# Attention product with two heads of both softmaxes in the rows, high and low factors in the columns, and its halves added in memory

## The chip, the core and the metric

One Trainium2 chip, one NeuronCore of it. The engines run their own instruction queues and meet at semaphores: TensorE (PE; its weight loads are PEld), VectorE (DVE), ScalarE (ACT), GpSimd (POOL) and SyncE (SP). DMAs are issued here by SyncE and by GpSimd. The metric is the device time of one execution in microseconds (us), the median of the runs.

## What is computed

Two blocks over the same x (2048 tokens, 1024 features), mixed by a gate per token. Block A is linear attention with 32 heads of 32 features; the feature map of a head is two softmaxes, of its projected query (or key) and of the negative. Block B is a gated MLP.

```
def _A_ref(x, wqkv, w_phi, wo):
    qkv = (x @ wqkv).reshape(B, S, 3, H, Dh).transpose(2, 0, 3, 1, 4)
    q, k, v = qkv[0], qkv[1], qkv[2]
    pq = einsum("bhsd,hdf->bhsf", q, w_phi); pk = einsum("bhsd,hdf->bhsf", k, w_phi)
    phi_q = concatenate([softmax(pq), softmax(-pq)], axis=-1)
    phi_k = concatenate([softmax(pk), softmax(-pk)], axis=-1)
    kv = einsum("bhsf,bhsd->bhfd", phi_k, v)
    z  = einsum("bhsf->bhf", phi_k)
    num = einsum("bhqf,bhfd->bhqd", phi_q, kv)
    den = einsum("bhqf,bhf->bhq", phi_q, z)[..., None] + 1e-6
    return (num / den).transpose(0, 2, 1, 3).reshape(B, S, D) @ wo
def _B_ref(x, w_gate, w_up, w_down):
    return (gelu(x @ w_gate) * (x @ w_up)) @ w_down
g = sigmoid((x * gate_w).sum(-1, keepdims=True))
return g * _A_ref(...) + (1 - g) * _B_ref(...)
```

## The kernel before

All matrix products work on float32r operands split into a high and a low part (`high` on ScalarE, `low` on VectorE, lines 420 to 424). A product takes three passes, high·high, high·low and low·high (`PASSES`), so 12 matmuls of 128x128 weights by 512 columns make a contraction of 512.

The program has three stages. The first (0 to some 460 us) makes keys and values, their feature map, and the sums `kv` and `z` of each head, which go to memory as `kz`. `finish_kv` (line 238) and `finish_z` (line 255) lay them out by partitions. The second, the *unit stage* (from 463 to 1691 us), makes everything that the last stage multiplies by `wo` and `w_down`: the gated MLP products (`left_mlp`) and the attention result (`left_att`). The third (from 1691 us, line 1088) multiplies those and adds up the output.

The unit stage handles the 2048 tokens in two halves. Gate, up and folded query weights are taken in pairs of 128 columns, and each pair is one *unit* of kind "g", "u" or "q": 30 units in the first half, 32 in the second. A unit is a seven-product scheme for a 2x2 block product (`unit`, line 765): seven products k = 0 to 6 of 12 matmuls. `mine.insert` (line 542) says where the query units stand among the others: in the first half before the change at places 2, 9, 16 and 23 (`7 * m + 2`). The results of a unit are taken out of PSUM at fixed slots after it (`results`, line 747); those of "u" and "q" units go through one of three `hidden` tiles (line 476) to memory by a DMA of GpSimd (`spill`, line 133, and line 732).

The order of instructions on TensorE, VectorE, ScalarE and SyncE is written out by a planner in the program text. `run_slot` (line 450) is called once behind each product. It has a budget of VectorE and ScalarE time per slot (`SLOT` = 2.65 us, plus 1.0 where an attention product was put in, less 0.6 of ScalarE for moves) and emits pieces of *streams*: Python generators that yield (not before slot, due slot, VectorE cost, ScalarE cost). A piece that is due is emitted whatever the budget; others are emitted while budget is left. A piece with a due slot of `NEVER` comes last.

Attention is such a stream without due slots (`attention`, line 838, called from `background`, line 817). For each of 32 *products* (half, group g of four heads, block j of 512 tokens) it loads the projected query from memory (`load_query`, line 831, one DMA of SyncE), transposes 32x32 blocks so that the features of a head lie along the free dimension, takes max and min, subtracts, applies Exp with scale 1 and -1 on ScalarE (line 872), sums, divides by the denominator and the gate, transposes back, and splits into high and low (`pts`). For j = 0 it also builds the block-diagonal factor `kbs` of the four heads from `kz`. `between` interleaves the sums of x for the second half and its reload (`second_half`).

The matmuls of a product are put into `fillers` and issued behind product k = 1 or k = 4 of a unit (line 801 on, in `unit`): `attend` (line 902) multiplies the block-diagonal factors of the two softmaxes by the two halves of `pts`, in three passes each, into one PSUM tile `misc`, evicts it into a `hidden` tile on ScalarE, and spills it to `left_att`. `free[0]` is False from the time a product is handed to `fillers` until it is issued; the stream waits for it before it overwrites `pts`, and, for j = 0, before it overwrites `kbs` (one buffer). What is left of the streams behind the last unit is emitted by `drain` (line 621), ahead of the third stage.

The first stage's and the third stage's loops are the same before and after, but for the layout of `kv` and `z`.

Of the kernel before, what the change touches and what calls it, by code (L numbers as in the profile page):

```python
# [16 lines left out]
P = 128  # L17
# [14 lines left out]
def tile_gated_mix(ctx: ExitStack, tc: tile.TileContext, x, xT, wkT, wqT, wv, w_phi, wo,  # L32
# [33 lines left out]
    for j in range(4):  # L66
        nc.vector.memset(mask[32 * j:32 * j + 32, j, :], 1.0)
    logit = keep.tile([P, S // P], F32, name="logit")
# [77 lines left out]
    with tc.tile_pool(name="kw", bufs=1) as kw, tc.tile_pool(name="kp", bufs=1) as kp, \  # L146
# [91 lines left out]
        def finish_kv(hh, pkv):  # L238
# [10 lines left out]
            for h in range(4):  # L249
                q = h % 2  # L250
                nc.scalar.activation(kv_c[32 * h:32 * h + 32, 4 * hh:4 * hh + 4],
                                     by_head[32 * q:32 * q + 32, :, h // 2, :, q], AF.Copy)
            yield

        def finish_z(hh, s, zacc, pz):
            nc.tensor.matmul(pz, ones, zacc[:, s].rearrange("p h f -> p (h f)"), start=True, stop=True)
            z4 = pz.rearrange("p (g h f) -> p g h f", g=4, h=4)
            for h in range(4):
                q = slice(32 * h, 32 * h + 32)
                nc.scalar.activation(zb[q, 4 * hh:4 * hh + 4, s], z4[q, :, h, :], AF.Copy)  # L260
# [177 lines left out]
    with tc.tile_pool(name="xa", bufs=1) as xa, tc.tile_pool(name="fp", bufs=1) as fp, \  # L438
# [5 lines left out]
        SLOT, NEVER = 2.65, 10 ** 9  # L444
# [227 lines left out]
        start(weights(0, 0, "g", 1))  # L672
# [92 lines left out]
        def unit(n, half, kind, m, before):  # L765
# [6 lines left out]
            for k in range(7):  # L772
# [30 lines left out]
                run_slot(7 * n + k, 1.0 if fill else 0.0, 0.6 * (moved + fill))  # L803
# [27 lines left out]
        def load_query(half, g, j):  # L831
            nc.sync.dma_start(work[:, 4], query[half][g][j])
            if j == 0:
                shared["z"] = fp.tile([P, 2, 2, 32], F32, tag="kz", name="kz", bufs=1)
                for i in range(2):
                    nc.sync.dma_start(shared["z"][:, i], kz[i][:, g])

        def attention(jobs, between):
# [4 lines left out]
            while more:  # L843
# [4 lines left out]
                e, f, x = blocks(e2), blocks(f2), work[:, 7].rearrange("p (a b) -> p a b", b=32)  # L848
                if j == 0:
                    while not free[0]:  # L850
                        yield now[0] + 1, NEVER, 0.0
                    yield now[0], NEVER, 0.5
                    kb = fp.tile([P, 2, 4, 32], F32, tag="kb", name="kb", bufs=1)
                    for s in range(2):
                        nc.vector.tensor_tensor(kb[:, s], z[:, 0, s:s + 1, :].to_broadcast([P, 4, 32]), mask, OP.mult)
                    kbs = shared["kbs"] = fp.tile([P, 2, 2, P], F32R, tag="kbs", name="kbs", bufs=1)
                    kb2 = kb.rearrange("p s a b -> p s (a b)")
                    high(kbs[:, 0], kb2)
                yield now[0], NEVER, 2.1
                nc.vector.transpose(work[:, 7], work[:, 4])  # L860
                mm = fp.tile([P, 2, 16], F32, tag="mm", name="mm", bufs=1)
                nc.vector.tensor_reduce(mm[:, 0, :], x, AX.X, OP.max)
                nc.vector.tensor_reduce(mm[:, 1, :], x, AX.X, OP.min)
                yield now[0], NEVER, 1.6
                if j == 0:
                    low(kbs[:, 1], kb2, kbs[:, 0])
                kbs = shared["kbs"]
                nc.vector.tensor_tensor(e, x.unsqueeze(1).to_broadcast([P, 2, 16, 32]),
                                        mm.unsqueeze(3).to_broadcast([P, 2, 16, 32]), OP.subtract)
                yield now[0] + 1, NEVER, 0.0, 2.0  # L870
                for s in range(2):
                    nc.scalar.activation(e2[:, s], e2[:, s], AF.Exp, scale=1.0 - 2 * s)  # L872
                st = fp.tile([P, 4, 2, 16], F32, tag="st", name="st", bufs=1)
                r, t, d, k = (st[:, i] for i in range(4))
                yield now[0] + 1, NEVER, 1.5
# [5 lines left out]
                yield now[0], NEVER, 2.0  # L881
                nc.vector.tensor_tensor(t, t, r, OP.mult)
                nc.vector.scalar_tensor_tensor(d[:, 0], t[:, 0], 1e-6, t[:, 1], OP.add, OP.add)
                nc.vector.reciprocal(d[:, 0], d[:, 0])
                c = 8 * half + 4 * j
                nc.vector.tensor_tensor(d[:, 0], d[:, 0], g_at[:, c:c + 4].rearrange("p c q -> p (c q)"), OP.mult)
                nc.vector.tensor_tensor(k, r, d[:, 0:1, :].to_broadcast([P, 2, 16]), OP.mult)
# [4 lines left out]
                pts = fp.tile([P, 2, 2, BLK], F32R, tag="pts", name="pts", bufs=1)  # L892
                nc.vector.transpose(wide[1], wide[0])
                yield now[0] + 1, NEVER, 0.0, 1.05
                high(pts[:, 0], f2)
                more = bool(jobs) and now[0] > jobs[0][0] and not (between and now[0] >= between[0][0] - 7)
                if more:
                    load_query(*jobs[0][1:])
                yield now[0] + 1, NEVER, 1.25
                low(pts[:, 1], f2, pts[:, 0])  # L900

                def attend(half=half, g=g, j=j, kbs=kbs, pts=pts):
                    po = misc()
                    for s in range(2):
                        for i, (a, q) in enumerate(PASSES):
                            nc.tensor.matmul(po, kbs[:, a, s, :], pts[:, q, s, :], start=s == 0 and i == 0,  # L906
                                             stop=s == 1 and i == 2)
                    h = hidden()
                    nc.scalar.activation(h, po, AF.Copy)
                    spill(h, left_att[half], j, g)  # L910
# [4 lines left out]
                fillers.append(attend)  # L915

# [257 lines left out]
```

## Time and profile before

| | us |
|---|---|
| median of three runs | 2383.89 (2383.17 to 2384.68) |
| the profiled execution, its time | 2383.34 |
| its span, first to last instruction | 2381.5 |
| unit stage, 467 to 1691 us: TensorE busy | 1222.98 |
| the same: VectorE, ScalarE, GpSimd busy | 897.80, 617.67, 133.25 |
| granted TensorE clock | 1.00 throughout |

Each row of a group names line, engine, operation, output<-inputs, shapes and count, then busy time and the mean of one in ns, then the idle time of the engine ahead of it and what ended that. A row of the timeline has start and length in us. A row of waits reads "who <- for whom: us in total, times, longest". Lengths of matmuls hold their modelled end, so the distance of two starts is what a matmul takes of TensorE.

### The profile page before, as it was taken

The numbers are of one execution on the slowest core, as the hardware profiler recorded it, in microseconds if no ns is written. First come the engines' busy times: TensorE is split into PE (matmuls) and PEld (weight loads), VectorE is DVE, ScalarE is ACT, GpSimd is POOL, SyncE is SP. The second block draws the span as 40 slices with busy tenths as digits, with TensorE's granted clock in tenths as the row PEclk, the third lists the DMA queues.
The fourth block names the chain that finished last, engine by engine and source line by source line (L and its number), as shares of the span: only waits on it lengthen the run. The fifth ranks groups of instructions, "written<-read, shape, count | busy, mean of one in ns | idle before, by whom it ended". The sixth has DMA issues, their size and how long they took to land.

```text
span 2381.5 us, 28170 instructions
## 1 busy us (share of the span) xinstructions
PE 2372.2 (100%) x10689; PEld 1969.3 (83%) x10689; DVE 1746.3 (73%) x2183; ACT 991.6 (42%) x1286; POOL 142.2 (6%) x266
## 2 busy tenths in 40 slices
PE   9999999999999999999999999999999999999999
PEld 8888888788888888888888888888888888888887
DVE  7877868858777777777767676777574878777773
ACT  4323332435445444555555555555443222323221
POOL 0000000011111121110001000000000000000000
PEclk9999999999999999999999999999999999999999
DMA  5112333544444556474444444444685767978774
GB/s 179 47 47 84 98 115 100 180 174 146 179 170 149 194 199 229 171 254 140 138 133 158 142 134 133 153 138 135 240 292 182 252 223 264 327 260 316 261 267 135
DMA packets 154360, 425.10 MB, mean 179 GB/s; under 512 B 21360, under 2 KB 21360, under 8 KB 154224
## 3 DMA queue, kind: packets, MB, share of 16 engines
q1 hardware_dynamic: 127872, 336.64, 42.6%
q0 software_dynamic: 25312, 86.52, 9.4%
q8 instruction: 84, 1.38, 0.2%
q14 instruction: 52, 0.43, 0.1%
q10 hardware_dynamic: 1040, 0.13, 0.0%
HBM read 328.34 MB, written 94.90 MB: 178 GB/s over the span
## 4 chain that ended last, share of the span: by engine, by line
PE 79%; DVE 0%; ACT 0%; issue 0%; ACTq 0%; DVEq 0%
PE po L1088 29%; PE a L744 21%; PE c L744 14%; PE b L744 7%; PE p L744 7%; PE misc L906 2%; DVE x L1048 0%; ACT L872 0%; DVE x L888 0%; DVE tyz L424 0%; ACT x L872 0%; DVE st L876 0%; DVE x L879 0%; ACT tyz L421 0%; DVE v L424 0%
## 5 line engine op out<-in xcount | busy, mean ns | idle before, releaser
L200 PE MATMUL pd<-wkv,x 128*128 128x512 f32 x1536 | 361.3, 392 | 0.0
L200 PEld LDWEIGHTS pd<-wkv,x 128*128 128x128 f32 x1536 | 284.8, 188 | 58.1 <-issue 1.0
L1088 PE MATMUL po<-tw,wgu 128*128 128x512 f32 x1344 | 309.8, 389 | 0.0
L1088 PEld LDWEIGHTS po<-tw,wgu 128*128 128x128 f32 x1344 | 252.3, 188 | 52.4
L421 ACT ACTIVATE wgu<-stage 128x1024 fp32r<-128x1024 f32 x147 | 155.2, 1057 | 291.0 <-PE po L1088 225.1
L424 DVE TENSOR_TENSOR wgu<-stage,wgu 128x1024 fp32r<-128x1024 f32 x147 | 179.6, 1222 | 123.7 <-ACT wgu L421 123.5
L424 DVE TENSOR_TENSOR tyz<-stage,tyz 128x1024 fp32r<-128x1024 f32 x126 | 153.0, 1215 | 41.8 <-ACT tyz L421 41.8
L421 ACT ACTIVATE tyz<-stage 128x1024 fp32r<-128x1024 f32 x126 | 132.7, 1053 | 115.6 <-DVE stage L569 64.3
L744 PE MATMUL a<-s,tyz 128*128 128x512 f32 x744 | 179.4, 390 | 0.9 <-DVE tyz L424 0.4
L744 PE MATMUL a<-x,wgu 128*128 128x512 f32 x744 | 178.7, 389 | 0.0
L744 PE MATMUL p<-s,tyz 128*128 128x512 f32 x744 | 178.7, 389 | 0.0
L744 PE MATMUL c<-x,wgu 128*128 128x512 f32 x744 | 178.7, 389 | 0.0
L744 PE MATMUL b<-s,tyz 128*128 128x512 f32 x744 | 178.7, 389 | 0.0
L744 PE MATMUL c<-x,tyz 128*128 128x512 f32 x744 | 178.7, 389 | 0.0
L744 PE MATMUL a<-s,v 128*128 128x512 f32 x744 | 178.7, 389 | 0.0
L744 PEld LDWEIGHTS a<-s,tyz 128*128 128x128 f32 x744 | 139.4, 188 | 31.0 <-DVE tyz L424 1.3
L744 PEld LDWEIGHTS p<-s,tyz 128*128 128x128 f32 x744 | 139.6, 188 | 29.1
L744 PEld LDWEIGHTS a<-x,wgu 128*128 128x128 f32 x744 | 139.6, 188 | 29.0
L744 PEld LDWEIGHTS c<-x,tyz 128*128 128x128 f32 x744 | 139.6, 188 | 29.0
L744 PEld LDWEIGHTS c<-x,wgu 128*128 128x128 f32 x744 | 139.6, 188 | 29.0
L744 PEld LDWEIGHTS a<-s,v 128*128 128x128 f32 x744 | 139.6, 188 | 29.0
L744 PEld LDWEIGHTS b<-s,tyz 128*128 128x128 f32 x744 | 139.6, 188 | 29.0
(176 smaller groups left out, 3423.7 us busy)
## 6 DMA issues: line engine op xcount, KB each, us to landing
stage<-lm SPq DMA_DIRECT2D x98, 512.0 KB, 3.6
sr<-in_w_down SPq DMA_DIRECT2D x84, 512.0 KB, 5.8
sl<-lm SPq DMA_DIRECT2D x70, 512.0 KB, 4.5
lm<-h POOLq DMA_DIRECT2D x112, 256.0 KB, 2.5
stage<-in_w_gate SPq DMA_DIRECT2D x43, 512.0 KB, 3.9
stage<-in_w_up SPq DMA_DIRECT2D x43, 512.0 KB, 4.2
stage<-la SPq DMA_DIRECT2D x28, 512.0 KB, 4.3
tg<-stage POOLq DMA_DIRECT2D x26, 512.0 KB, 3.1
```

The costliest lines, as they stand in the source:

```text
L200: nc.tensor.matmul(ps[m], xb[b, kc // 4][:, a, kc % 4, t * P:(t + 1) * P], w[:, e, m * 512:(m + 1) * 512], start=kc == 0 and i == 0, stop= ...
L421: nc.scalar.activation(dst, src, AF.Copy)
L424: nc.vector.tensor_tensor(dst, src, dst_h.bitcast(F32), OP.subtract)
L744: nc.tensor.matmul(dst, w[:, h, 4 * part + kc, :], xq[:, e, kc, :], start=first and kc == 0 and i == 0, stop=kc == 3 and i == 2, skip_grou ...
L906: nc.tensor.matmul(po, kbs[:, a, s, :], pts[:, q, s, :], start=s == 0 and i == 0, stop=s == 1 and i == 2)
L1088: nc.tensor.matmul(ps[c], ls[:, a, m, c * P:(c + 1) * P], rs[:, e, m], start=opens and m == 0 and j == 0, stop=closes and m == 1 and j == 2)
```

## The change

The 32 rows of one head's one softmax, four heads deep, made the contraction of 128 before, once for each softmax. Now the rows hold two heads, each with both softmaxes, and a group of four heads is two pairs. For each pair the weights are 128 columns wide: 64 hold the high part of the pair's block-diagonal `kv`, 64 the low part, so that one matmul gives high and low results in different rows of PSUM. Two matmuls (high and low of `pts`) for each of two pairs make a product: four matmuls for six. The four combinations are all computed, low·low included. Rows of high and low results must be added: both PSUM tiles are evicted to two `hidden` tiles, the high rows are written to `left_att` by two plain DMAs, and the low rows are added to them in memory by two accumulating DMAs. This is the new stream `attended`, which is due in the slot behind the product.

So that both softmaxes lie in rows, the query is loaded twice, by four DMAs of 32 rows, and a ScalarE copy with a scale of 1 or -1 by row (`sign`) makes the negative ahead of the transpose. One max and one Exp over 1024 columns replace max and min and two Exps over 512. The denominators of the two softmaxes lie in neighbouring groups of 32 rows, and four small copies on VectorE bring them together. `kbs` has two buffers, and the wait for `free[0]` at j = 0 goes. The next query load is issued one slot earlier. `SLOT` becomes 2.72, the addition for a filled slot 0.9 and its ScalarE deduction goes; the query units of the first half stand at places 0, 5, 10 and 15, and the first unit is now whatever stands first.

```
+    pair_mask = keep.tile([P, 2, 32], F32, name="pair_mask")
+    nc.vector.memset(pair_mask, 0.0)
+    for j in range(2):
+        nc.vector.memset(pair_mask[64 * j:64 * j + 64, j, :], 1.0)
+    sign = keep.tile([P, 1], F32, name="sign")
+    for j in range(4):
+        nc.vector.memset(sign[32 * j:32 * j + 32], 1.0 - 2 * (j % 2))
...
-            for h in range(4):
-                q = slice(32 * h, 32 * h + 32)
-                nc.scalar.activation(zb[q, 4 * hh:4 * hh + 4, s], z4[q, :, h, :], AF.Copy)
+            z4 = pz.rearrange("p (g w h f) -> p g w h f", g=4, w=2, h=2)
+            for h in range(2):
+                q = slice(64 * h + 32 * s, 64 * h + 32 * s + 32)
+                nc.scalar.activation(zb[q, 4 * hh:4 * hh + 4], z4[q, :, :, h, :], AF.Copy)
...
-        SLOT, NEVER = 2.65, 10 ** 9
+        SLOT, NEVER = 2.72, 10 ** 9
...
-                mine.insert((0, 7, 12, 19)[m] if half else 7 * m + 2, (half, "q", m))
+                mine.insert((0, 7, 12, 19)[m] if half else 5 * m, (half, "q", m))
...
-        start(weights(0, 0, "g", 1))
+        start(weights(0, *units[0]))
...
-                run_slot(7 * n + k, 1.0 if fill else 0.0, 0.6 * (moved + fill))
+                run_slot(7 * n + k, 0.9 if fill else 0.0, 0.6 * moved)
...
-            nc.sync.dma_start(work[:, 4], query[half][g][j])
+            rows = query[half][g][j].rearrange("(w h f) t -> h f w t", w=2, h=2)
+            for h in range(2):
+                for s in range(2):
+                    nc.sync.dma_start(work[64 * h + 32 * s:64 * h + 32 * s + 32, 4:6], rows[h])
...
+                yield now[0], NEVER, 0.0, 1.05
+                nc.scalar.activation(e2, e2, AF.Copy, scale=sign)
+                yield now[0] + 1, NEVER, 1.3 if j else 1.8
                 if j == 0:
-                    while not free[0]:
-                        yield now[0] + 1, NEVER, 0.0
-                    yield now[0], NEVER, 0.5
...
-                    kbs = shared["kbs"] = fp.tile([P, 2, 2, P], F32R, tag="kbs", name="kbs", bufs=1)
+                    kbs = shared["kbs"] = fp.tile([P, 2, 2, 64], F32R, tag="kbs", name="kbs", bufs=2)
...
-                yield now[0], NEVER, 2.1
-                nc.vector.transpose(work[:, 7], work[:, 4])
+                nc.vector.transpose(wide[1], wide[0])
+                yield now[0], NEVER, 2.5
                 mm = fp.tile([P, 2, 16], F32, tag="mm", name="mm", bufs=1)
-                nc.vector.tensor_reduce(mm[:, 0, :], x, AX.X, OP.max)
-                nc.vector.tensor_reduce(mm[:, 1, :], x, AX.X, OP.min)
+                nc.vector.tensor_reduce(mm, f, AX.X, OP.max)
...
-                for s in range(2):
-                    nc.scalar.activation(e2[:, s], e2[:, s], AF.Exp, scale=1.0 - 2 * s)
+                nc.scalar.activation(e2, e2, AF.Exp)
...
+                for q in range(4):
+                    nc.vector.tensor_copy(k[32 * q:32 * q + 32], t[32 * (q ^ 1):32 * (q ^ 1) + 32])
+                nc.vector.scalar_tensor_tensor(d, t, 1e-6, k, OP.add, OP.add)
+                nc.vector.reciprocal(d, d)
...
                 def attend(half=half, g=g, j=j, kbs=kbs, pts=pts):
-                    po = misc()
+                    po = [misc(), misc()]
                     for s in range(2):
-                        for i, (a, q) in enumerate(PASSES):
-                            nc.tensor.matmul(po, kbs[:, a, s, :], pts[:, q, s, :], start=s == 0 and i == 0,
-                                             stop=s == 1 and i == 2)
-                    h = hidden()
-                    nc.scalar.activation(h, po, AF.Copy)
-                    spill(h, left_att[half], j, g)
+                        for q in range(2):
+                            nc.tensor.matmul(po[s], kbs[:, s].rearrange("p a b -> p (a b)"), pts[:, q, s, :],
+                                             start=q == 0, stop=q == 1)
+                    start(attended(po, half, g, j))
                     free[0] = True
...
+        def attended(po, half, g, j):
+            yield now[0] + 1, now[0] + 1, 0.0, 1.2
+            dst = left_att[half][g // 4][j, g % 2, :, g // 2 % 2, :]
+            hs = [hidden() for _ in po]
+            for h, p in zip(hs, po):
+                nc.scalar.activation(h, p, AF.Copy)
+            rows = [slice(64 * s, 64 * s + 64) for s in range(2)]
+            for s in range(2):
+                nc.gpsimd.dma_start(dst[rows[s]], hs[s][rows[s]])
+            for s in range(2):
+                nc.gpsimd.dma_start(dst[rows[s]], hs[s][rows[1 - s]], accum_op=OP.add)
```

More of the change, by code (lines that the diff above doesn't have):

```diff
@@ L898, in attention @@
                     load_query(*jobs[0][1:])
+                pts = fp.tile([P, 2, 2, BLK], F32R, tag="pts", name="pts", bufs=1)
+                yield now[0] + 1, NEVER, 0.0, 1.05
+                high(pts[:, 0], f2)
                 yield now[0] + 1, NEVER, 1.25
```

42 lines of the change are left out of this document (19 added, 23 removed).

## Prediction

> **What bounds the kernel now.** I read the page's engine totals first, then who kept TensorE waiting, then the chain of waits.
>
> ```profile
> span 2381.5 us, 28170 instructions
> PE 2372.2 (100%) x10689; PEld 1969.3 (83%) x10689; DVE 1746.3 (73%) x2183; ACT 991.6 (42%) x1286; POOL 142.2 (6%) x266
> PE c L703 <- DVE h L651: 1.6, 1, 1.6
> PE pd L154 <- DVE ones L149: 1.2, 1, 1.2
> PE pg L190 <- DMA early<-in_wkT: 1.2, 1, 1.2
> PE a L744 <- DVE tyz L424: 0.4, 1, 0.4
> PE a L744 <- ACT c L777: 0.4, 1, 0.4
> PE po L1088 29%; PE a L744 21%; PE c L744 14%; PE b L744 7%; PE p L744 7%; PE misc L906 2%; DVE x L1048 0%; ACT L872 0%; DVE x L888 0%; DVE tyz L424 0%; ACT x L872 0%; DVE st L876 0%; DVE x L879 0%; ACT tyz L421 0%; DVE v L424 0%
> ```
>
> TensorE is busy for 2372.2 of 2381.5 us and waited for others five times, 4.8 us in all. Being busy does not prove much for pipelined matmuls, so the chain matters more: it runs through matmuls in nearly all of the part after 474 us, and 2% of the span are the attention matmuls of line 906, the ones that the change cuts. Nothing else is long on it. A matmul taken out should shorten the span by its own time, provided that the work around it keeps up. So two questions: what is one matmul worth, and does the cover hold?
>
> The first is read off TensorE's timeline at the last attention product:
>
> ```profile
> 1676.05 2.88 PE L744 MATMUL a<-s,v 128*128 128x512 f32 x12
> 1678.77 1.52 PE L906 MATMUL misc<-pts,kbs 128*128 128x512 f32 x6
> 1680.13 2.88 PE L744 MATMUL c<-x,wgu 128*128 128x512 f32 x12
> ...
> 1691.01 11.04 PE L1088 MATMUL po<-tyz,wgu 128*128 128x512 f32 x48
> ```
>
> Twelve matmuls start 2.72 us before the next group (1676.05 to 1678.77), six start 1.36 us before it (1678.77 to 1680.13): 226.7 ns each, back to back. I call 2.72 us a slot; a unit has seven. The same rows show something that matters below: this last attention product lies behind product k=4 of the last unit, the last place where one can be put, 12 us before the final stage begins at 1691.01.
>
> **The change part by part: TensorE.** Lines 904 to 907 issue two softmaxes times three passes, six matmuls for each (half, group, j). After the change it is two head pairs times high and low of the query factor, four. How many times:
>
> ```profile
> L906 PE MATMUL misc<-pts,kbs 128*128 128x512 f32 x192 | 48.7, 389 | 0.0
> L909 ACT ACTIVATE h<-misc 128x512 f32<-128x512 f32 x32 | 19.2, 599 | 100.5 <-PE misc L906 100.5
> ```
>
> 192 / 6 = 32 products, so 64 matmuls go: 64 x 0.2267 = 14.5 us. Their shape stays 128x128 by 512. The Trainium skill ("TensorE: Matmul & The Clock Gate", section "Back-to-back issue gap") gives about 131 ns as the sustained spacing of 512-column matmuls; by it the gain would be 64 x 0.131 = 8.4 us. This trace measures 226.7 ns for the same instruction in the same loop, so the measurement decides, and that rule gets no chance of its own.
>
> **VectorE, ScalarE and the queues.** Per product (32 of them), from these rows of the unit stage, 467 to 1691 us (the last row is from before it):
>
> ```profile
> L893 DVE STREAM_TRANSPOSE x<-x 128x1024 f32<-128x1024 f32 x32 | 39.6, 1238 | 0.0
> L876 DVE TENSOR_REDUCE st<-x 128x32 f32<-128x1024 f32 x32 | 38.9, 1216 | 47.4 <-ACT x L872 47.4
> L872 ACT ACTIVATE x<-x 128x512 f32<-128x512 f32 x64 | 37.0, 625 | 0.4
> L421 ACT ACTIVATE pts<-x 128x1024 fp32r<-128x1024 f32 x32 | 33.8, 1056 | 5.5 <-DVE x L893 5.5
> L860 DVE STREAM_TRANSPOSE x<-x 128x512 f32<-128x512 f32 x32 | 22.6, 706 | 0.1
> L862 DVE TENSOR_REDUCE mm<-x 128x16 f32<-128x512 f32 x32 | 22.0, 686 | 1.1
> L863 DVE TENSOR_REDUCE mm<-x 128x16 f32<-128x512 f32 x32 | 21.7, 677 | 0.0
> L877 DVE RECIPROCAL st<-st 128x32 f32<-128x32 f32 x32 | 11.3, 353 | 1.1
> L884 DVE RECIPROCAL st<-st 128x16 f32<-128x16 f32 x32 | 8.1, 253 | 1.1
> ...
> L406 DVE COPY g_at<-g_a 32x16 f32<-32x16 f32 x16 | 2.8, 173 | 0.2
> ```
>
> VectorE: the first transpose grows from 706 to 1238 ns (+0.53); max and min (0.686 + 0.677) become one reduce of 1024 columns, 1.22 (-0.14); four small copies come in, by the nearest row (32x16) 0.173 each (+0.69); the second reciprocal doubles (+0.10). The block-diagonal factor is built from half as many elements; I count it as nothing. Sum +1.2 us, 38 us over the stage. ScalarE: a sign copy of 128x1024 (+1.06, the row of pts), one Exp of 1024 for two of 512 (1.06 for 2 x 0.578 = 37.0 / 64 each, -0.10), one more eviction (+0.60): +1.6 us, 50 us. Against this stands the sum over the same stretch:
>
> ```profile
> sum 1224.00, PE 1222.98 PEld 1011.63 DVE 897.80 ACT 617.67 POOL 133.25; mean PE 101.91 PEld 84.30 DVE 74.82 ACT 51.47 POOL 11.10
> ```
>
> VectorE goes from 898 to about 936 of some 1210 us (77%), ScalarE from 618 to 668 (55%). Neither is a bound in the mean, so all of this costs nothing while TensorE covers it. Without that cover it would be 38 us.
>
> GpSimd and SyncE issue more: four spills instead of one per product, and four query loads instead of one.
>
> ```profile
> L135 POOL DMA_DIRECT2D la<-h x32 | 17.4, 543 | 273.0 <-ACT h L909 260.5 <-ACT kbs L421 12.3 <-issue 0.2
> L832 SPq DMA_DIRECT2D x<-q x32: 319/320/338, 530.6 to 1637.6; - x32
> la<-h POOLq DMA_DIRECT2D x32, 256.0 KB, 2.3
> DMA to landing us min/median/max: 2.3/4.0/7.9
> ```
>
> 96 issues of 0.543 us are 52 us more on a GpSimd that works 133 of 1224; 96 of 0.32 are 31 us on SyncE. Both fit. The query load moves: it is now issued behind the emission of the second transpose, one slot earlier, so SyncE waits there for that transpose with that slot's stage loads behind it, up to 2.7 us later than now; the weight they carry is due two slots or more after its load. And a ScalarE instruction (the sign copy), no longer a VectorE one, now waits for that load.
>
> The accumulating spill is the new wait. GpSimd must see the plain spills land before it issues the adding ones, with the spills of lines 721 and 731 queued behind. Who waits for that: the three `hidden` tiles, of which two are now held at once. The held time: two evictions 1.2, four issues 2.2, two landings one after the other. No row shows an accumulating transfer. The nearest, the plain spill, lands in 2.3; the longest of any transfer that touches this tensor took 7.9. So 8.0 us at best and 19 at worst; I take 8.0 to 9, since half as many bytes move each time. The tile comes round again 3 slots (8.2 us) later at the earliest, where the writer is VectorE's last result of the unit, due 2 slots before TensorE wants its bank. So by the low end nothing is lost. By the high end 11 us less the 5.4 of slack, about 6 us, would be lost in some 9 products (32, half of them behind k=1, 35 of 62 units writing such tiles): 50 us.
>
> The four small copies on VectorE last 0.7 us in all (row of line 406), so whatever they do to GpSimd, by rows the chain grows by at most that, to 8.7 us, past the 8.2; this is part of the chance given to the second rival below. The Trainium skill ("SBUF — State Buffer", section "SBUF: two separate sides") speaks against them: a float32 copy on VectorE locks GpSimd out of writing descriptors, and a 620 ns transfer took 3100 ns beside one; with 2.5 us more at each of two issues in a row, an estimate from that page, the chain would be 13 us and the second rival would cost little under 1 us per product. No run here shows it yet.
>
> Edits before the unit stage (more memsets, fewer copies in `finish_z`) are under 1 us, on engines that wait for loads there. I count them as nothing, at most 0.5.
>
> **The planner.** Attention is emitted as a stream with no due time into what the slots' budgets leave. Now it ends exactly in the last place. Twelve products lie before the second half's reload of x (580 to 1034 us), twenty behind it:
>
> ```profile
> 580.52 1.52 PE L906 MATMUL misc<-pts,kbs 128*128 128x512 f32 x6
> ...
> 1111.65 1.52 PE L906 MATMUL misc<-pts,kbs 128*128 128x512 f32 x6
> ```
>
> (1678.77 - 1111.65) / 19 = 29.85 us; less 1.36, over 2.72: 10.5 slots each. If it gets longer, products slip past the last unit, where TensorE waits for the chain. The change adds one forced slot (a sign copy ahead of the transpose) and 0.6 us of planned VectorE time, some 0.4 slot at the 1.65 us per slot that the second half's other streams leave. It takes away the wait of each j=0 for the product before it (`kbs` has two buffers now): fills go only behind k=1 and k=4, so that wait is 1 to 3 slots, mean 1.75, every second product: -0.9. The larger budget (2.72 for 2.65) gives 0.07 x 10.5 / 1.65 = -0.4. Sum +0.1 slot per product, by the ends of that wait from -0.5 to +0.5. Against it stands an earlier start: the first query unit is unit 0 instead of 2, 14 slots. Over 32 products that covers 0.44 slot each. I take it that the stream fits, by about ten slots.
>
> **The sum.** The profiled execution took 2383.34 us, its span 2381.5. -14.5 from TensorE, +0.5 for small waits: 2369.3. The median of the runs shown, 2383.89, is 0.55 higher: 2369.9, rounded to 2370.
>
> **The rivals.** *The stream ends late* (the other side). Place: behind the last unit, ahead of the final stage. Price: 2.72 us per slot of lateness, since TensorE's queue holds the late product ahead of line 1088. It decides from 14.5 / 2.72 = 5.3 slots: at the +0.5 end, 32 x 0.5 - 14 = 2 slots, 2375; if the forced slot is paid and none of the j=0 wait comes back (+1.0), 18 slots late, 2370 + 49 = 2419. For it: the last product now lies in the last place. Against: the added buffer and the earlier start. *The accumulate chain stalls VectorE and then TensorE*: about 1 us for each of 9 to 32 products, 2379 for nine at 1 us to the bound above, 2420. For it: 8.0 against 8.2 us is no margin. Against: VectorE idles a quarter of the stage, and no spill has held it yet. *The query load holds ScalarE*: it comes up to 2.7 us later than before for one slot's worth of work, 32 x at most 0.3 us if a tenth reaches TensorE, 2380. Against: TensorE waited 0.4 us for ScalarE in the whole run.
>
> **How the numbers follow.** Forecast (all covered) 0.56, at 2368 to 2373. Stream late 0.22: 0.08 still faster, 0.03 no change, 0.11 slower. Accumulate chain 0.15: 0.09, 0.04, 0.02. Query load 0.07: 0.05, 0.01, 0.01. A difference under 0.2% (4.8 us) can't be told from none here, so faster means below 2379.1: 0.56 + 0.08 + 0.09 + 0.05 = 0.78; same 0.08; slower 0.14. The range takes the forecast from 2367.5 (2383.9 - 14.5, less the 1.6 us wait of line 703, should the new first unit end it, rounded down) up to 2381, where the mild ends of the three rivals lie; beyond it is left the late stream and the bound of the accumulate chain, under 0.2.
>
> **What would show it.** Right: line of the attention matmul x128 and about 1.36 - 0.45 = 0.91 us at each; TensorE's waits in total below 7 us; the last product more than a unit before the final stage. Wrong: a gap on TensorE just ahead of the first po matmul (late stream); VectorE's or ScalarE's writes of h waiting for la transfers (accumulate chain); ScalarE waiting for x<-q (query load).

## The result, and the profile after

The changed kernel takes 2392.89 us (median of six runs, 2388.36 to 2396.19) beside 2383.97 (2383.17 to 2384.68) of the kernel before: a ratio of 1.0037 with a 95% interval of 1.0024 to 1.005. It is slower by 8.9 us, where 14 us less had been forecast. The profiled execution took 2388.36 us, the shortest of the six, so the views below account for only 4.4 of the 8.9 us.

The page of the changed kernel: its span, the engine totals, the first part of the chain that ended last; then the view of TensorE's waits, which reads "who <- for whom: us in total, times, longest".

```profile
span 2386.6 us, 28661 instructions
PE 2365.3 (99%) x10625; PEld 1959.1 (82%) x10625; DVE 1778.3 (75%) x2302; ACT 1026.2 (43%) x1322; POOL 218.2 (9%) x362
PE 66%; DVE 6%; issue 4%; DMA 2%; ACT 2%; POOL 0%; SPq 0%; DVEq 0%; ACTq 0%; POOLq 0%
```

```profile
PE a L751 <- DVE h L726: 3.5, 1, 3.5
PE p L751 <- ACT x L764: 3.3, 3, 2.1
PE a L751 <- DVE tyz L431: 3.3, 4, 1.3
PE pd L161 <- DVE ones L156: 2.5, 1, 2.5
PE b L751 <- ACT b L786: 1.7, 3, 1.2
...
```

64 matmuls fewer ran (10689 to 10625), as planned. But TensorE, which waited for others for 4.8 us, now waits, with the smaller rows of this view, for 16.7 in this one execution, 14.2 of them from 466 us on, for several different writers. In the chain that ended last, matmuls had 79% of the span before and no other engine as much as 1%; now matmuls have 66%, VectorE 6%, ScalarE 2% and DMAs 2%. The edges of the unit stage on TensorE's timeline, after the change, give the loss in one subtraction: the last attention product and the first row of the final stage are

```profile
1638.73 1.07 PE L918 MATMUL misc<-pts,kbs 128*128 128x512 f32 x4
1696.75 3.56 PE L1110 MATMUL po<-tyz,wgu 128*128 128x512 f32 x15
```

The final stage began at 1691.01 before and begins at 1696.75 now. The 14.5 us of matmuls are gone from the stretch ahead of it, so about 20 us of new losses have come in. The waits that the view counts are 14.2 us of that stretch, for 2.4 before. The rest goes with the gaps too: idle time is counted from a modelled end (2.88 us after the start, where the next group otherwise starts 2.72 after it), and behind some gaps the matmuls are slower (last section). The question of the experiments is where the gaps come from.

Two views of all engines between 467 and 1700 us show candidates. First who waited for transfers (the changed kernel), then the same rows of the kernel before, then SyncE's wait for the attention transpose (before, and after).

```profile
ACT wgu L428 <- DMA stage<-in_w_up: 21.1, 6, 6.1
ACT wgu L428 <- DMA stage<-in_w_gate: 16.6, 5, 4.8
DVE h L726 <- DMA la<-h: 13.0, 3, 8.7
ACT v L428 <- DMA stage<-in_w_gate: 11.3, 3, 4.3
ACT v L428 <- DMA stage<-in_w_up: 7.4, 2, 4.0
...
ACT x L860 <- DMA x<-q: 4.6, 6, 1.3
```

```profile
ACT wgu L421 <- DMA stage<-in_w_up: 5.2, 2, 2.7
ACT wgu L421 <- DMA stage<-in_w_gate: 4.4, 2, 2.8
ACT v L421 <- DMA stage<-in_w_up: 0.8, 1, 0.8
```

```profile
SPq L832 <- DVE x L893: 184.3, 26, 15.6
```

```profile
SPq L842 <- DVE x L904: 352.5, 27, 22.2
```

ScalarE's waits for the gate and up weight loads (into `stage`, read in line 428, before in line 421) have grown from 10.4 us (5.2 + 4.4 + 0.8) to 56.4 (21.1 + 16.6 + 11.3 + 7.4); VectorE waits for spills of `hidden` tiles, which it did not before; and SyncE, which issues the weight loads, stands twice as long in front of the query load.

The theories, by the letters that the expectations use: **A**, the accumulate chain holds the `hidden` tiles; **B**, the planner's slots are too full with `SLOT` at 2.72; **C**, the query load, issued a slot earlier, blocks SyncE and with it the weight loads; **D**, the reload of x for the second half starts late and crowds with everything else. All kernels that start from the changed one are compared below both with the kernel before (ratio) and with the changed kernel's 2392.89.

### The profile page after: what moved, and what is told of

Its sections match the earlier page's. It is cut to its first block, busy times and chain, and to the rows that moved or that the text cites. A ratio compares the mean times of both kernels' runs of the same rounds, so it can differ in the third digit from the quotient of the medians.

```text
span 2386.6 us, 28661 instructions
## 1 busy us (share of the span) xinstructions
PE 2365.3 (99%) x10625; PEld 1959.1 (82%) x10625; DVE 1778.3 (75%) x2302; ACT 1026.2 (43%) x1322; POOL 218.2 (9%) x362
## 4 chain that ended last, share of the span: by engine, by line
PE 66%; DVE 6%; issue 4%; DMA 2%; ACT 2%; POOL 0%; SPq 0%; DVEq 0%; ACTq 0%; POOLq 0%
PE po L1110 29%; PE a L751 16%; PE c L751 10%; PE p L751 5%; PE b L751 5%; PE misc L918 1%; DVE tyz L431 1%; DMA la<-h 1%; DMA stage<-in_w_gate 1%; DVE x L888 1%; DVE st L885 1%; DVE wgu L431 0%; DMA stage<-in_w_up 0%; ACT x L881 0%; ACT L881 0%
```

## The experiments

**A: no adding DMAs (n1), and adding DMAs later (n4).** The first leaves out the two accumulating transfers, and with them the low rows of the attention result; the second lets the planner place them two slots later.

```
-            for s in range(2):
-                nc.gpsimd.dma_start(dst[rows[s]], hs[s][rows[1 - s]], accum_op=OP.add)
```

> The two adding DMAs of each product are left out, so the attention result has the high rows alone. Theory A (the adding DMAs hold two of the three hidden tiles and GpSimd's queue, VectorE and ScalarE wait for a free tile, TensorE for them): most of the 21 us of gaps in TensorE's unit stage go, 2374 to 2381 us. Theory B (the planner's slots are too full, so weights come late): little changes, 2388 to 2393 us. Theory C (stage loads late behind the query loads in SyncE's queue): as B.

```
+            yield now[0] + 2, now[0] + 2, 0.0
             for s in range(2):
                 nc.gpsimd.dma_start(dst[rows[s]], hs[s][rows[1 - s]], accum_op=OP.add)
```

> The adding DMAs are issued two slots (5.4 us) later, when the plain ones have landed, so that GpSimd does not stand still in front of them. If GpSimd's blocked queue is what costs (Theory A's second half): 2382 to 2388 us. If the tile's holding time is what costs: the tiles are held as long or longer, 2390 to 2400 us. Theories B and C: 2391 to 2394 us.

Without the adding DMAs: 2389.89 us (1.0026, interval 1.0016 to 1.0035), 3.0 less than the changed kernel, far from the 2374 to 2381 that theory A gave. With them later: 2391.9 (1.0034, 1.0022 to 1.0046), 1.0 less. The intervals of both overlap that of the changed kernel (1.0024 to 1.005); u3 below measures the adding DMAs more clearly. The chain of theory A is there, and the trace of the changed kernel shows one case whole. These are rows of its timeline on GpSimd, TensorE and VectorE (start, length, engine, operation, and in brackets the idle time before it with what ended it):

```profile
942.00 1.08 POOL L935 DMA_DIRECT2D la<-h  x2
...
945.86 0.87 POOL L937 DMA_DIRECT2D la<-h  x1 [2.78 <-DMA la<-h]
...
954.39 0.69 DVE L726 TENSOR_TENSOR h<-a,x 128x512 f32<-128x512 f32 x1 [8.71 <-DMA la<-h]
955.14 4.53 PE L751 MATMUL a<-x,wgu 128*128 128x512 f32 x12 [3.48 <-DVE h L726]
```

Two plain spills at 942, the first adding one when a plain one has landed, the second at 947.01, and VectorE gets a tile at 954.39: 12.4 us from the first issue, with 8.7 of them spent idle. TensorE loses 3.48 us by it. But VectorE met this wait three times in the whole stage (13.0 us), not 9 to 32 times, and without the chain 6 of the 9 us of loss stay. A is a part, not the cause. A fourth `hidden` tile (run n2), the other way to test it, gave no result: the pool would take 59.625 kb per partition, and 58.5625 are left.

**B: a smaller budget (n3).**

```
-        SLOT, NEVER = 2.72, 10 ** 9
+        SLOT, NEVER = 2.60, 10 ** 9
```

> The planner's budget per slot is 2.60 us instead of 2.72, nothing else; the attention stream ended 45 us ahead of the last unit, so it can afford it. Theory B: VectorE's queue runs less far behind, waits for tyz (weights) and x go, 2378 to 2385 us. Theory A: the waits for hidden tiles stay, 2389 to 2394 us. Theory C: 2390 to 2394 us.

2389.38 us (1.0022, 1.0012 to 1.0031), 3.5 less, with an interval that overlaps that of the changed kernel, and outside the 2378 to 2385 that theory B gave. The small gaps near 555 and 810 us, which come back in nearly all kernels with 2.72, are gone, others have come (TensorE waited 6.0 us for ScalarE's x of line 764, four times). The same kernel also began its reload of x 11 us earlier (1027.51 instead of 1038.82 us), so the run does not separate B from D.

**C and D: the query load and the reload of x (q1 to q4).** Before these, I read what SyncE does in a slot in which it is blocked. Rows of SyncE, VectorE and ScalarE in the timeline of the changed kernel:

```profile
582.62 0.33 SPq L51 DMA_DIRECT2D stage<-in_w_gate  x1
...
600.11 1.23 DVE L904 STREAM_TRANSPOSE x<-x 128x1024 f32<-128x1024 f32 x1
...
601.41 1.74 SPq L842 DMA_DIRECT2D x<-q  x4
...
603.20 0.94 SPq L51 DMA_DIRECT2D stage<-in_w_gate  x2
604.24 1.98 SPq L51 DMA_DIRECT2D stage<-in_w_up  x2
608.10 1.06 ACT L428 ACTIVATE wgu<-stage 128x1024 fp32r<-128x1024 f32 x1 [4.83 <-DMA stage<-in_w_gate]
```

SyncE issues nothing between 582.95 and 601.41: the query load stands at its head and waits for the transpose that reads the tile it overwrites, and that transpose comes late because VectorE's stream is late. The weight loads behind it, four of them, go out at 603 to 606, and ScalarE, which needs the first at 603, gets it at 608. VectorE waits 4.67 us for ScalarE's copy of that weight (to 609.19) and then works without a pause up to the write of `h` at 618.52; ScalarE needs that for its x of line 764, and TensorE, which needs the x, is short by 0.77 us at 619.89. q1 issues the load one slot later again, as before the change; it differs from the changed kernel in nothing but SyncE's order:

```
-                more = bool(jobs) and now[0] > jobs[0][0] and not (between and now[0] >= between[0][0] - 7)
-                if more:
-                    load_query(*jobs[0][1:])
                 pts = fp.tile([P, 2, 2, BLK], F32R, tag="pts", name="pts", bufs=1)
                 yield now[0] + 1, NEVER, 0.0, 1.05
                 high(pts[:, 0], f2)
+                more = bool(jobs) and now[0] > jobs[0][0] and not (between and now[0] >= between[0][0] - 7)
+                if more:
+                    load_query(*jobs[0][1:])
```

> The changed kernel with the query load issued behind the high copy of pts again, one slot later, as before the change; TensorE, VectorE and ScalarE have the same order, only SyncE's differs. Theory C (SyncE stands in front of the second transpose, stage loads queue behind it, weights come late): SyncE's wait for that transpose falls from 352 us towards the 184 of before, ScalarE's waits for stage loads from 61 us to under 30, and the time to 2384 to 2389 us. Theory A (hidden tiles) and Theory D (the reload of x for the second half starts 11 us late because an attention product runs past its slot): no change, 2391 to 2394 us.

q2 keeps attention products away from the 18 slots ahead of the reload instead of 7, so that the reload is not held back by a product that runs past it:

```
-                elif jobs and now[0] >= jobs[0][0]:
+                elif jobs and now[0] >= jobs[0][0] and not (len(between) == 1 and now[0] >= between[0][0] - 18):
...
-                more = bool(jobs) and now[0] > jobs[0][0] and not (between and now[0] >= between[0][0] - 7)
+                more = bool(jobs) and now[0] > jobs[0][0] and not (between and now[0] >= between[0][0] - (18 if len(between) == 1 else 7))
```

> The changed kernel, but no attention product is begun in the 18 slots ahead of the reload of x (second_half), so the 13th product comes behind it. Theory D: the gaps of TensorE between 1054 and 1080 us (5.5 us in the profile) go, 2385 to 2389 us; the last product still lies ahead of the last unit. Theories A and C: under 2 us of change, 2390 to 2394 us.

q3 has both edits:

> Both edits. If C and D are separate causes their gains add up: 2378 to 2385 us. If one of them is no cause, it equals the other run within 1.5 us. What then is left above 2369.5 us belongs to the hidden tiles (3 us by the run without adding DMAs) and to slots planned too full.

q4 is the kernel *before* with the early query load alone:

```
-                yield now[0] + 1, NEVER, 0.0, 1.05
-                high(pts[:, 0], f2)
                 more = bool(jobs) and now[0] > jobs[0][0] and not (between and now[0] >= between[0][0] - 7)
                 if more:
                     load_query(*jobs[0][1:])
+                yield now[0] + 1, NEVER, 0.0, 1.05
+                high(pts[:, 0], f2)
```

> The kernel before, with the one edit that its query load is issued one slot earlier, in front of the high copy of pts. Theory C: SyncE waits longer for the transpose and TensorE gets gaps from late stage loads, 2385.5 to 2392 us. If the early load harms only together with the rest of the change: 2383 to 2385 us, no difference.

| kernel | us | ratio to before (95%) | against the changed one | SyncE waits for the transpose |
|---|---|---|---|---|
| q1, load back | 2386.64 | 1.0006 (0.9997 to 1.0016) | -6.3 | 260.6 us |
| q2, reload first | 2390.42 | 1.0028 (1.0016 to 1.0039) | -2.5 | 371.6 us |
| q3, both | 2380.84 | 0.9986 (0.9976 to 0.9995) | -12.1 | 275.8 us |
| q4, before with the early load | 2383.83 | 0.9999 (0.999 to 1.0008) | | 382.8 us |

C holds: q1 lies in the range that theory C gave, its interval is clear of that of the changed kernel, and ScalarE's waits for gate and up weights fall from 56.4 us to 25.6. TensorE's waits for `tyz` (3.3 us above) and the gap of 619.89 are gone from q1's trace. The 6.3 us themselves rest on the medians: the two profiled executions, the shortest of the one kernel and a long one of the other, differ by 0.8 us. q4 sets a limit: in the kernel before, the same early load lets SyncE wait for 382.8 us and ScalarE for 28.3 instead of 10.4, and costs nothing (2383.83 beside 2384.11). So the move costs only together with the rest of the change; that the difference is slack, VectorE and ScalarE having more work in the changed kernel, is argued and not shown.

D does not show in q2 alone: 2.5 us less, with overlapping intervals, lies in the range that the theories other than D gave. It shows once C is undone: q3 is 5.8 us below q1, and their intervals do not overlap. Behind the reload, where q1 still has gaps of 2.08 and 3.58 us on TensorE, q3 has one of 0.48. These are SyncE's first two pairs of loads of the reload, in the timeline before, after, and (the second pair) in q3; and what SyncE waited for with them after (line 528, between 1000 and 1085 us):

```profile
1027.68 1.14 SPq L521 DMA_DIRECT2D x<-in_xT  x2
1035.66 0.82 SPq L521 DMA_DIRECT2D raw<-xs  x2
```

```profile
1038.82 1.15 SPq L528 DMA_DIRECT2D x<-in_xT  x2
1048.66 0.82 SPq L528 DMA_DIRECT2D raw<-xs  x2
```

```profile
1019.43 1.14 SPq L528 DMA_DIRECT2D raw<-xs  x2
```

```profile
SPq L528 <- PE misc L918: 8.7, 1, 8.7
```

The second pair goes into `raw`, which takes the buffer of `pts`: it must wait for the last attention product ahead of the reload. That product ran at 1034.11 before, runs at 1047.56 now (there are 13 ahead of the reload for 12), and at 1007.83 in q3, where 12 stand ahead again. The stretch behind the reload, in rows of the window view (stretch, length, then busy time of PE, PEld, DVE, ACT and POOL, the granted clock, the DMA share, GB/s), first before, then after:

```profile
1050.00:1080.00 30.00, 30.00 (x134) 24.82 (x133) 25.50 (x30) 19.93 (x26) 3.34 (x7) 1.00 0.80 281
```

```profile
1050.00:1080.00 30.00, 26.68 (x109) 21.27 (x109) 23.72 (x27) 18.24 (x24) 4.73 (x8) 0.94 0.93 318
```

Here TensorE misses 25 matmuls of 134, 5.7 us at 226.7 ns each: it idles for 3.32 us (2.08 and 1.24), and the rest are slower matmuls at a granted clock of 0.94. The DMA engines are busy for 0.93 of the time; what the crowding itself costs was not separated. The two edits together give 12.1 us, more than 6.3 and 2.5: so the two faults are not independent. The trace of q2 shows a part of why. The two gaps of 2.08 and 1.24 us are gone from it, but TensorE's waits for `tyz`, which q1 does not have, have grown from 3.3 us to

```profile
PE a L751 <- DVE tyz L431: 5.4, 4, 1.7
```

so with the query load still early, other waits take up a part of what the early reload gives.

**The hidden tiles freed (s1, s2), the budget again (s3), the load later still (s4).** s1 is the changed kernel with the evictions going into a tile that takes over the buffer of `pts`, so the accumulate chain holds no `hidden` tile (and `pts` instead, which is needed later):

```
-                    free[0] = True
...
-            hs = [hidden() for _ in po]
+            spent = fp.tile([P, 2, 2, BLK], F32, tag="pts", name="spent", bufs=1)
+            hs = [spent[:, 0, i] for i in range(2)]
+            free[0] = True
```

> The changed kernel, but the two evictions go into the spent pts tile (its matmuls are done, it is not written again for some seven slots) instead of two hidden tiles; free[0] is set there, one slot later. Theory A's first half (tiles held through the chain of plain and adding DMAs): VectorE's waits for la transfers (13.0 us) go, and the time falls by 3 to 6 us, to 2387 to 2390 us. If GpSimd's blocked queue is what made those waits (lm spills behind it), or if they are not on the path: less than 1.5 us, 2391.5 to 2394 us.

s2 is s1's edit on q3:

> The same with the late query load and the reload of x first (the kernel that took 2380.8 us). If A, C and D add up: 2374 to 2378 us, and the 5.5 us gap at 947 to 954 us is gone; this would beat both kernels. If A is not separate: 2379 to 2382 us.

s3 is s2 with `SLOT` at 2.65:

> The same with SLOT at 2.65 us, as before the change. Theory B (slots planned too full): the small gaps after tyz and x go, 1 to 3 us faster than the run at 2.72, 2372 to 2376 us. Without B: within 1 us of it, or slower if products get late.

s4 is s2 with `load_query` behind `low(pts[:, 1], ...)`, one more slot later than before the change:

> As the second of these runs, with the query load one slot later still, behind the low copy of pts. Theory C in full (each slot in which SyncE stands in front of the transpose costs): SyncE's wait for the transpose falls from 276 us to under 200, 1 to 4 us faster than that run, 2371 to 2376 us. Against it: the sign copy on ScalarE waits longer for the query (x<-q, 2.9 us in that order), which would make it as fast or slower.

| kernel | us | ratio to before (95%) |
|---|---|---|
| s1, spent on the changed kernel | 2401.61 | 1.0069 (1.0054 to 1.0084) |
| s2, spent on q3 | 2379.71 | 0.998 (0.9971 to 0.9989) |
| s3, s2 with 2.65 | 2380.68 | 0.9986 (0.9977 to 0.9995) |
| s4, s2 with the load last | 2378.55 | 0.9978 (0.9968 to 0.9987) |

s1 came out on the wrong side, and shows D more sharply than q2 did. The reload's `raw` loads, which need the buffer of `pts`, now wait for the spills as well, and go out at 1059.37 us. SyncE's waits between 1000 and 1085 us in s1, and TensorE's timeline of s1 there:

```profile
SPq L528 <- DMA la<-spent: 16.1, 3, 12.3
```

```profile
1068.32 5.24 PE L751 MATMUL p<-s,tyz 128*128 128x512 f32 x12 [8.71 <-ACT x L764]
```

One gap of 8.71 us. On top of q3, where the reload is early, the same edit costs nothing and gains next to nothing: VectorE's waits for `la` transfers and the gap at 954 us go, but one of 2.72 us comes at 975.40. s2 is 1.1 below q3, s4 1.2 below s2, neither of them more than the intervals allow for chance. That puts s2 where A is no separate cause, and s4 above the 2371 to 2376 us that theory C in full gave. s4 differs from the kernel before beyond its interval, and from the changed kernel by 14.3 us; its waits of SyncE for the transpose fell from 276.2 us in s2 to 132.1, below those before the change. ScalarE's waits for the query rose from 1.2 to 16.2 us instead, and the 1.2 us between the two kernels are within chance, so the sum of SyncE's waits is no measure of their cost. s3 shows both ends of B: from 472 us on TensorE waits only 0.3 us for others in the whole unit stage, but with the smaller budget the stream ends late, and TensorE waits 6.2 us for `pts` of the last product, ahead of the final stage:

```profile
PE misc L918 <- ACT pts L428: 6.2, 1, 6.2
```

**What is left in s4 (u1, u2, u3).** s4 is still 9 us above the 2369.5 that 14.5 us less would give. u1 plans the denominator's piece at the 3.0 us that it takes, for 2.4:

```
-                yield now[0], NEVER, 2.4
+                yield now[0], NEVER, 3.0
```

> The kernel of 2378.55 us (spent tile, reload first, query load behind the low copy) with the planner told 3.0 us instead of 2.4 for the piece of small steps, which the profile shows to take 3.0. Theory B (slots planned too full; the gaps at 552 and 808 us, 1.6 us each, come from VectorE running behind): 2375 to 2377.5 us and those two gaps go. Without B: within 1 us of 2378.5.

u2 puts the query units of the first half back to places 2, 9, 16 and 23:

```
-                mine.insert((0, 7, 12, 19)[m] if half else 5 * m, (half, "q", m))
+                mine.insert((0, 7, 12, 19)[m] if half else 7 * m + 2, (half, "q", m))
```

> The same kernel of 2378.55 us with the query units of the first half at their old places (2, 9, 16, 23). If the new places of the units are what brings the gaps at 552, 808 and 970 us (query units and attention products fall on the dense slots): 2374 to 2377 us. If not: 2378 to 2381 us, and the stream ends some 14 slots later, still ahead of the last unit, since it had 45 us to spare.

u3 is s4 without the adding DMAs:

> The same kernel of 2378.55 us without the adding DMAs (the attention result has the high rows alone). If the accumulation still costs once the tiles are not hidden ones and the loads are on time (GpSimd's queue, DMA traffic): 2374 to 2377 us. If it is paid off: within 1 us of 2378.5, and what is left belongs to the planner.

| kernel | us | ratio to before (95%) |
|---|---|---|
| u1, true cost planned | 2393.87 | 1.0041 (1.0026 to 1.0056) |
| u2, old places | 2404.26 | 1.0089 (1.0072 to 1.0106) |
| u3, no adding DMAs | 2375.43 | 0.9966 (0.9953 to 0.9979) |

u1 and u2 miss both of their ranges: in both the stream is late, and the last product falls behind the last unit. u1 also leaves the gaps that it was to close (0.69 us at 555.38, 0.68 at 811.13). TensorE's timeline of u2 there:

```profile
1693.05 2.88 PE L751 MATMUL c<-x,tyz 128*128 128x512 f32 x12
1705.62 0.80 PE L918 MATMUL misc<-pts,kbs 128*128 128x512 f32 x1 [9.69 <-ACT pts L428]
1706.88 1.65 PE L918 MATMUL misc<-pts,kbs 128*128 128x512 f32 x3 [0.47 <-DVE pts L431]
1709.70 13.25 PE L1111 MATMUL po<-tyz,wgu 128*128 128x512 f32 x48 [1.17 <-ACT spent L933]
```

TensorE has nothing but the last product to do and waits for its ScalarE copy, then for its VectorE copy, then the final stage waits for PSUM to be emptied. This is the late stream that the prediction described, produced by undoing one part of the change. These three waits are 11.3 of the 25.7 us by which u2 is slower than s4; it has longer gaps earlier as well (3.02 us at 936.75). u3 puts the adding DMAs at 3.1 us (2378.55 to 2375.43; the kernel before took 2384.00 beside the one and 2383.65 beside the other), and no run of the one lies in the range of the other. n1's 3.0 agrees, so they seem to cost that much with or without the other faults.

## Why the prediction was wrong

**Right.** The saving on TensorE: 128 matmuls for 192, same durations. The row of the product's tile in the changed kernel (count, then shortest/median/longest ns):

```profile
L918 PE MATMUL misc<-pts,kbs x128: 389/389/389, 542.0 to 1639.4; 128*128 128x512 f32 x128
```

The busy sums: VectorE was put at about 936 us in the stage and ScalarE at 668, neither a bound; in the stretch from 467 to 1691 us they are 926 and 651 (GpSimd 209).

```profile
467.00:1691.00 1224.00, 1210.35 (x5302) 995.66 (x5301) 926.14 (x1309) 651.49 (x887) 208.64 (x341) 1.00 0.56 177
```

The late stream did not come at the end of this kernel. The last product is 58.0 us ahead of the final stage (1696.75 - 1638.73), where it was 12.2 ahead before. That is 45.8 us, some 17 slots, of slack where ten were worked out. u2 shows that the earlier places carry it. So the forecast had this wait right, and most of the chance that it gave to a slower kernel (0.11 of 0.14) lay on a rival that did not come; the kernel is slower for other reasons.

**The step that failed.** "It is now issued behind the emission of the second transpose, one slot earlier, so SyncE waits there for that transpose with that slot's stage loads behind it, up to 2.7 us later than now; the weight they carry is due two slots or more after its load." The place is right. The 2.7 us are too small, but not by much in the mean: against q1, the same kernel with the load back, SyncE waits 352.5 us for 260.6 over 27 loads, 3.4 us more for each, and 22.2 for 16.4 at the longest. What failed is the second half, the two slots (5.4 us) in hand. SyncE does not wait for the slot in which the planner emits the transpose but for VectorE to run it, and a piece without a due time runs long after it was emitted: SyncE stood 18.5 us before the load at 601.41, and the weight loads behind it came 4.83 us too late for ScalarE. The trace of before had the row that says so, and the prediction does not use it: 26 waits there, 7.1 us each in the mean and 15.6 at the longest, on a load issued a slot later. That is more than the two slots already, so the added wait had to be set against what the rest of the kernel can absorb. ScalarE's waits for gate and up weights rose from 10.4 to 56.4 us, and undoing this step alone (q1) takes them to 25.6 and gives 6.3 us back. The rival "query load holds ScalarE" named the wrong waiter too: the sign copy waited 4.6 us for the query, less than a tenth of the 56.4 for the weights behind it, and none of the signs that the prediction named looks at those loads.

**The step that was missing.** The stream was asked only whether it ends ahead of the last unit. It has a second deadline in its middle, the reload of x, and the prediction's own count of products before it held that number: "twelve products lie before the second half's reload". The earlier places that bring the slack at the end let a thirteenth product begin ahead of the reload and run past its time, so its loads go out 11 and 13 us late, with TensorE short by 5.7 us behind them. q3 over q1 gives 5.8 us (2386.64 to 2380.84) for this, and s1, where the reload is later still, is 8.7 above the changed kernel.

**A term of the wrong size.** The accumulate chain was put at 8.0 to 9 us with 19 as the bound, and a loss in nine products or more if it passed 8.2. It is 12.4 us in the one case that reaches TensorE, and VectorE meets it three times. The slack was mis-sized as well. Of a chain of 13 us the prediction's own terms would lose nothing (13 less 8.2 is 4.8, below its 5.4 of slack), where it says a little under 1 us; the 12.4 that came cost TensorE 3.48 us of idle time. An adding issue occupies GpSimd longer than a plain one, as the tile's rows show:

```profile
L935 POOL DMA_DIRECT2D la<-h x64: 534/547/562, 543.5 to 1640.8; - x64
L937 POOL DMA_DIRECT2D la<-h x64: 837/875/1219, 549.3 to 1643.6; - x64
```

64 times 0.33 us is 21 us; with the 133 of before and the prediction's 52 for new issues that makes 206 of the 209 us of GpSimd above. The cost is 3 us for the kernel (u3, and n1 agrees), a third of the least that this rival was priced at (nine products at 1 us). What the Trainium skill ("SBUF — State Buffer", section "SBUF: two separate sides") says of a float32 copy on VectorE that keeps GpSimd from writing descriptors is hardly tested here: no plain issue of the changed kernel ran beside one of the four new copies. Of the adding issues, the first of two from 627.91 on ran beside all four copies (from 627.90, 0.79 us), and the two took 1.74 us, 0.87 each, as elsewhere. Nearly all the others ran beside no copy and took as long, so the copies are not what makes them longer; what does was not separated.

**The sum.** The saving alone would give 2369.5 (2383.97 less 14.5; the forecast, with 0.5 for small waits, was 2370). The kernel took 2392.9, 23.4 us more. Of these 12.1 go with the query load and the reload (q3), 2.3 with the freed tile and the still later load (s4, each alone within the intervals), 3.1 with the adding DMAs (u3). The 5.9 that remain are open. In part they are gaps that the kernels with 2.72 and the new places share. s4 has them too:

```profile
555.74 3.03 PE L751 MATMUL b<-s,tyz 128*128 128x512 f32 x12 [0.68 <-ACT b L786]
```

and again at 811.39. The smaller budgets close them (n3, s3) but lose as much elsewhere, s3 by a late last product. Its waits at the end are 7.9 us (6.2, and with smaller rows 0.5 and 1.2); without them s3 would be at about 2373, an estimate that no run tested, and 2369.5 with the 3.1 of the adding DMAs is 2372.6. So slots planned too full are the likely source of the 5.9. That is argued, not shown; u1, which told the planner one true cost, did not close these gaps.

## What to carry to other kernels

Before a load is moved ahead in a queue, read how long its queue stands there now, from the trace, and not from the planner's slot: everything behind the waiting issue is late by that. The price depends on the rest of the kernel (the same move cost nothing in the kernel before and 6.3 us here). A stream without due times must be checked against each deadline that it interleaves with, not only against the end. The best kernel here, s4, keeps the change, takes both faults out and evicts into the spent `pts` buffer: 2378.55 us, 0.9978 of the time before.

## What the hardware showed

After a gap of some 2 us or more the next twelve matmuls of TensorE often took longer than twelve elsewhere. In the changed kernel the group at 955.14, after 3.48 us idle, starts 4.33 us before the next (959.47), for 2.72 elsewhere, and the granted clock of the stretch is 0.83:

```profile
950.00:960.00 10.00, 6.52 (x22) 4.92 (x21) 5.47 (x8) 1.69 (x3) 1.75 (x4) 0.83 0.93 309
```

So that gap costs some 1.6 us again. After 1.24 us idle (at 1075.54) the group took 2.87. But the length of the gap does not decide it. The same gap of 2.08 us stands in the changed kernel and in n1:

```profile
1058.87 4.54 PE L751 MATMUL p<-s,tyz 128*128 128x512 f32 x12 [2.08 <-ACT x L764]
```

```profile
1057.02 3.04 PE L751 MATMUL p<-s,tyz 128*128 128x512 f32 x12 [2.08 <-ACT x L764]
```

In the first the next group starts 4.37 us later, at a granted clock of 0.83 from 1054 to 1064 us; in the second 2.88 us later, at 1.00 in the same window. In s4 a group after 2.62 us idle (975.56) started 2.89 us before the next, at 1.00.
